# Turns of entry 1 and chunk 4 by 64-row halves, inside other small-matmul bursts

## The chip, the cores and the metric

One core of one Trainium2 chip runs the whole kernel. The metric is device time in microseconds; times shown are medians of several executions, and one execution was profiled.

Engine names in the profile: PE does matmuls (PEld its weight loads), DVE, ACT and POOL do elementwise work, SP and POOL issue DMA transfers. PE writes only to PSUM, which has eight banks here: five in the tensor `psA`, three in `psB`.

## The reference

Retention with decay per head, then a two-layer network on the tokens. Eight entries of 576 tokens, eight heads of 64; the network has 512 inputs and 2048 hidden units, on 4608 tokens.

```python
def _attn_ref(q, k, v) -> np.ndarray:
    scores = scale * np.matmul(q, k.transpose(0, 1, 3, 2))
    gamma = 1.0 - 2.0 ** (-5.0 - np.arange(H, dtype=np.float32))
    rel = pos[:, None] - pos[None, :]
    Dmat = np.where(rel >= 0, gamma[:, None, None] ** rel[None, :, :], 0.0)
    ret = scores * Dmat[None, :, :, :]
    return np.matmul(ret, v).astype(np.float32)
...
def _moe_ref(x, w_in, w_out) -> np.ndarray:
    h = x @ w_in
    g = h * (1.0 / (1.0 + np.exp(-1.702 * h)))
    return (g @ w_out).astype(np.float32)
```

## The kernel before

**Two kinds of work on PE.** The network is big matmuls: `hidden` (L765) makes one of 16 hidden tiles for a chunk of 512 tokens, 4 matmuls of 128x512; `hidden_half` (L780) does two tiles for half a chunk, 8 matmuls of 128x256; `project` (L801) adds 4 hidden tiles to 128 output rows, 4 matmuls of 128x512. Retention is small matmuls on 64-wide heads, and it runs in bursts between the big ones. Its result, scaled, goes to `xT`, which `hidden` reads.

**Retention by pieces.** Entry 0 is done in five chunks of its own (128 rows four times, then 64): chunk 4 is the short one. For a chunk n, `scores` (L463) and `mask_s` (L475) give masked scores in `sm`; `values` (L483) gives the values times scores, adds to the running state (`add_state`) and adds the part that comes from the state of earlier chunks (`add_inter`); `evac_z` (L542) copies the state out of PSUM, `evac_o` (L553) writes `xT`. The other entries are done in 21 wide steps m of 192 tokens each, in `burst(m_out, m_in)` (L626): it brings in scores and state of step m_in and takes out the values of step m_out, the values in two phases of which the second waits for the first. After it on DVE: `evac_wide` (L721) writes `xT`, `mask_wide` (L731) writes `sm`, `state_wide` (L740) adds the state to `zacc`, three operations, and a cast (ACT or DVE) makes `zw`, which the next burst's output side reads. `step(m)` is `burst(m, m+1)` and what goes with it.

**Turns.** Scores need q and k with the head dimension across partitions. From entry 2 on, a DMA transposes them (`turn_dma`, L567). For chunk 4 and the five chunks of entry 1 (n = 5 to 9), PE does it: `turn` (L562) is `transposes` (L409), 8 matmuls of 128x128 against the identity, and `evac_t` (L420), one ACT copy of 128x1024 to `qk`.

**Order.** All is written out by hand. A call records an operation on its engine's queue; each engine runs its queue in that order. The recorder (class `Rec`, L44) makes an operation wait for the last writer and the readers of what it touches, named by keys. PSUM is named by bank: "S" is `psA` banks 0 and 1, "O" bank 2, "Z" bank 3, "W" bank 4, and `psB` has ("H", 0), ("H", 1) and "U". An operation that names a bank waits for the last operation of every other engine that named the same bank, whichever columns each of them uses:

```python
        for key in ps:
            for e, o in self.ps.get(key, {}).items():
                if e != eng:
                    deps.append(o)
```

`state_wide` names "S", "W", "Z" and "O" in each of its three DVE operations (L751, L755).

`run(units, between)` (L1005) records units (one `project`, `hidden` or `hidden_half` each) and, after unit i, what `between[i]` lists; a unit with a step behind it also waits for what the step reads. The first such call (L1040) has the 16 project units of chunk 0, unit 4g + r for group g and rows r; r = 0 adds up in bank "O" over units 0, 4, 8 and 12. The next (L1047) has eight `hidden_half` units of chunk 1's first half, whose tokens come from entry 0's chunk 4 and from step 0. Loads are issued by POOL (`load`, L213) in order; from a point on each waits until the sixth load before it has landed.

## Time and profile before

| what | us |
|---|---|
| median of 3 runs (lowest, highest) | 297.17 (296.97, 298.06) |
| the profiled execution | 296.6 |
| its span | 294.8 |
| PE busy | 289.6 |
| POOL, ACT, DVE busy | 150.1, 126.6, 124.0 |
| first project unit of chunk 0 begins | 29.93 |
| first hidden unit of chunk 1 begins | 48.38 |
| first project unit of chunk 1 begins | 57.50 |

The span runs from the first instruction to the last. Lines in the timeline give start, length, engine, line, operation and tiles, array shape (rows*columns of PE in use), the moving operand's shape and a count; consecutive equal instructions are merged. Matmuls overlap: a group's length includes the tail of its last one, so the time that a group takes is read from one start to the next.

### The profile page before, as it was taken

The page shows a single profiled execution, that of the slowest core. Times are in us where ns is not written, and L with a number is a line of the kernel's source. Part 1 is how long each engine was busy: PE and PEld are TensorE (multiplying, and loading weights), DVE is VectorE, ACT ScalarE, POOL GpSimd, SP SyncE. Part 2 cuts the span into 40 slices and gives each one's busy share as a digit, 9 for nine tenths or more (in the row PEclk, how much of TensorE's full clock was granted, in tenths as well). Part 3 has the DMA queues.
Part 4 walks back from the last instruction along what each step waited for, and adds up shares of the span by engine and source line. Part 5 has one row for each costly group of instructions (what it writes and reads, how often), then busy time and mean ns, then how long its engine had stood idle before and what let it go on. Part 6 is the DMA issues. An engine that isn't in the chain of part 4 may idle for free.

```text
span 294.8 us, 7772 instructions
## 1 busy us (share of the span) xinstructions
PE 289.6 (98%) x3434; PEld 148.9 (51%) x3434; DVE 124.0 (42%) x221; ACT 126.6 (43%) x212; POOL 150.1 (51%) x202
## 2 busy tenths in 40 slices
PE   7999999999999999999999999999999999999996
PEld 3664556758544544554454544544444544444444
DVE  6899284644545443642424415235325504100012
ACT  7767338517175224531454045403650366036600
POOL 8958879999869879769968960000000000000000
PEclk9999999999999999999999999999999999999999
DMA  9999999999999999999999996008610200020012
GB/s 188 166 201 185 172 172 197 160 142 146 185 156 204 141 143 192 189 141 119 141 220 147 134 222 102 4 0 111 180 29 0 109 36 2 2 107 36 0 58 87
DMA packets 151746, 36.31 MB, mean 123 GB/s; under 512 B 141344, under 2 KB 147232, under 8 KB 151712
## 3 DMA queue, kind: packets, MB, share of 16 engines
q0 software_dynamic: 114224, 17.84, 90.9%
q1 hardware_dynamic: 37488, 17.97, 30.9%
q8 instruction: 27, 0.44, 0.6%
q14 instruction: 7, 0.06, 0.1%
HBM read 36.70 MB, written 9.44 MB: 157 GB/s over the span
## 4 chain that ended last, share of the span: by engine, by line
PE 93%; POOL 2%; DMA 2%; DVE 1%; issue 1%; POOLq 0%
PE psB L804 40%; PE psB L771 36%; PE psB L788 5%; PE psA L666 2%; PE psA L638 2%; DMA st_k<-in_k_dram 2%; PE psA L680 2%; PE psA L654 1%; PE psA L804 1%; PE psA L830 1%; POOL st_v L223 1%; POOL st_k L223 1%; PE psA L415 1%; DVE xT L557 0%; DVE sm L480 0%
## 5 line engine op out<-in xcount | busy, mean ns | idle before, releaser
L804 PE MATMUL psB<-w_out_sb,gT 128*128 128x512 bf16 x544 | 122.1, 379 | 0.0
L771 PE MATMUL psB<-xT,w_in_sb 128*128 128x512 bf16 x492 | 108.9, 379 | 0.0
L776 ACT ACTIVATE gT<-psB 128x512 bf16<-128x512 f32 x123 | 73.5, 597 | 38.7 <-PE psB L771 38.6
L804 PEld LDWEIGHTS psB<-w_out_sb,gT 128*128 128x128 bf16 x544 | 51.8, 98 | 60.3 <-DVE sm L735 0.4
L771 PEld LDWEIGHTS psB<-xT,w_in_sb 128*128 128x128 bf16 x492 | 47.4, 98 | 56.5
L724 DVE TENSOR_TENSOR xT<-psA,gq 128x768 bf16<-128x768 f32 x21 | 20.1, 957 | 113.9 <-PE psA L654 113.9
L236 POOL DMA_DIRECT2D st_k<-in_k_dram x70 | 52.9, 786 | 8.6 <-DMA st_k<-in_k_dram 3.0
L236 POOL DMA_DIRECT2D st_v<-in_v_dram x70 | 52.5, 779 | 4.5 <-DMA st_v<-in_v_dram 3.7
L813 ACT ACTIVATE osb<-psB 128x512 f32<-128x512 f32 x23 | 13.7, 597 | 71.9 <-PE psB L804 71.9
L223 POOL DMA_DIRECT2D st_q<-in_q_dram x36 | 32.3, 898 | 9.9 <-DMA st_q<-in_q_dram 6.0
L394 DVE TENSOR_TENSOR st_v<-st_v,vfac 128x512 bf16<-128x512 bf16 x38 | 24.8, 682 | 1.9 <-DMA st_v<-in_v_dram 1.9
L753 DVE TENSOR_TENSOR zacc<-zacc,psA 128x256 f32<-128x256 f32 x49 | 20.5, 418 | 7.5 <-PE psA L666 6.3
L735 DVE TENSOR_TENSOR sm<-psA,maskw 128x768 bf16<-128x768 f32 x21 | 19.9, 947 | 0.0
L788 PE MATMUL psB<-xT,w_in_sb 128*128 128x256 bf16 x128 | 15.0, 273 | 0.0
L816 DVE COPY osb<-psB 128x512 f32<-128x512 f32 x3 | 2.1, 691 | 29.7 <-PE psB L804 29.7
L788 PEld LDWEIGHTS psB<-xT,w_in_sb 128*128 128x128 bf16 x128 | 12.2, 98 | 1.7
L813 ACT ACTIVATE posi<-psB 128x512 f32<-128x512 f32 x8 | 4.8, 597 | 17.7 <-PE psB L804 17.7
L638 PE MATMUL psA<-sm,st_v 64*64 64x64 bf16 x504 | 11.7, 195 | 0.3
L666 PE MATMUL psA<-st_v,st_k 64*64 64x64 bf16 x448 | 11.8, 199 | 0.0
L666 PEld LDWEIGHTS psA<-st_v,st_k 64*64 64x64 bf16 x448 | 7.6, 105 | 8.3 <-issue 7.8
L794 ACT ACTIVATE gT<-psB 128x512 bf16<-128x512 f32 x16 | 9.4, 599 | 5.0 <-PE psB L788 5.0
L654 PE MATMUL psA<-qk,zw 64*64 64x64 bf16 x448 | 11.0, 194 | 0.0
(114 smaller groups left out, 172.2 us busy)
## 6 DMA issues: line engine op xcount, KB each, us to landing
out_dram<-osb SPq DMA_DIRECT2D x27, 256.0 KB, 4.2
st_k<-in_k_dram POOLq DMA_DIRECT2D x57, 64.0 KB, 6.7
st_v<-in_v_dram POOLq DMA_DIRECT2D x57, 64.0 KB, 6.5
st_q<-in_q_dram POOLq DMA_DIRECT2D x28, 128.0 KB, 7.9
w_out_sb<-in_moe_w_out_dram POOLq DMA_DIRECT2D x4, 512.0 KB, 11.3
out_dram<-posi SPq DMA_DIRECT2D x8, 256.0 KB
w_in_sb<-in_moe_w_in_dram POOLq DMA_DIRECT2D x3, 512.0 KB, 8.2
gT<-in_q_dram SPq DMA_DIRECT2D x2, 512.0 KB, 4.3
```

The source lines that it names most:

```text
L223: paced(R.op("POOL", lambda e, d=d, s=s: e.dma_start(d, s), w=[(nm, sl, c)], dma=(nm, sl, c), own=pace()))
L236: paced(R.op("POOL", lambda e: [e.dma_start(d, s) for d, s in parts], w=[(nm, sl, c)], dma=(nm, sl, c), parts=2, own=pace()))
L394: R.op(eng, lambda e: e.tensor_tensor(t, t, f, ALU.mult), r=[("vfac", min(b, 1))], w=[("v", sl, c)])
L666: i = e.matmul(psA[half(j), bank, off + 64 * t : off + 64 * t + 64], rows_of(st_k, m_in, g, u, h), rows_of(st_v, m_in, g, u, h), start=(t ...
L724: R.op("DVE", lambda e: e.tensor_tensor(xT[:, :, t0 : t0 + 192].rearrange("p (u j) n -> p u j n", u=2), psA[:, 2:4, 0:384].rearrange("p u ...
L735: R.op("DVE", lambda e: e.tensor_tensor(o, i, k, ALU.mult), r=["maskw"], w=[("sm", si(m))], ps=["S"])
L753: R.op("DVE", lambda e, to=to, src=src, was=was: e.tensor_tensor(to, was, src, ALU.add), r=[("zacc", (blk - 1) % 3)], w=[("zacc", blk)], p ...
L771: i = e.matmul(bank, w_in_sb[:, a, 128 * f : 128 * f + 128], xT[:, a, 512 * c : 512 * c + 512], start=(a == 0), stop=(a == 3))
L776: R.op("ACT", lambda e: e.activation(gT[c % 2][:, f, :], bank, AF.Gelu_apprx_sigmoid), w=[("gT", c % 2, f)], ps=[key])
L788: m = e.matmul(bank[:, 256 * i : 256 * i + 256], w_in_sb[:, a, 128 * (f + i) : 128 * (f + i) + 128], xT[:, a, a0 : a0 + 256], start=(a == ...
L804: i = e.matmul(bank, gT[c % 2][:, f, 128 * r : 128 * r + 128], w_out_sb[:, f, :], start=(f == 0), stop=(f == NF - 1))
L813: R.op("ACT", lambda e: e.activation(osb[m], bank, AF.Copy), w=osb_keys[m], ps=[key])
```

## The change

- `transposes`, `evac_t`, `scores`, `mask_s` and `values` use only the rows that a chunk of entry 0 has: for chunk 4, 64 rather than 128.
- A new `turn_halves` does a turn as 16 transposes, each of 64 rows by 128 columns, the two halves into two banks, with one ACT copy. A new `turn_tail` does chunk 9: the low half of q and of k into bank "O", the high half of k into bank "W", with two ACT copies.
- Turn 4 now runs with the state of chunk 3, which moves from the hidden units of chunk 0 to behind project unit 1. Scores 4 run with turn 5 behind unit 5 (before: units 3 and 5). Turn 6 runs with the values of chunk 4 behind unit 8 (before: units 7 and 5). Burst 0 moves from unit 9 to 10, step 0 from 13 to 15, with turns 7 and 8 between its two phases (before: units 12 and 15). Burst 1 moves from hidden unit 1 to 3 and has turn 9 behind it (before: unit 0); step 1 moves from 6 to 7.
- The regroupings of `w_in` columns 2 and 3 on DVE stand behind units 1 and 11 (before: 5 and 11); the memsets of chunk 4's unused rows move behind `evac_o` of chunk 3.

```diff
+        def turn_halves(n, at, x0=0):
+            bank, keys = at
+            to = bank.bitcast(BF16)[:, :, x0 : x0 + 2 * HP * 64].rearrange("p r (x n) -> p r x n", n=64)
+            def fn(e):
+                for a, t, nm, sl, c in sides(n):
+                    for hp in range(HP):
+                        for r in range(2):
+                            i = e.matmul(to[:, r, HP * a + hp, :],
+                                         t[half(r), sl, c, 128 * hp : 128 * hp + 128],
+                                         ident[half(r), half(r)], is_transpose=True)
+                return i
+            R.op("PE", fn, r=["ident"] + [(nm, sl, c) for a, t, nm, sl, c in sides(n)], ps=keys)
+            o = qk[n % NQK].ap().rearrange("p a h (r n) -> p r (a h) n", r=2)
+            R.op("ACT", lambda e: e.activation(o, to, AF.Copy),
+                 w=[("qk", n % NQK, 0), ("qk", n % NQK, 1)], ps=keys)
+
+        def turn_tail(n):
+            keys = ["O", "W"]
+            (_, tq, nmq, sl, c), (_, tk, nmk, _, _) = sides(n)
+            low = psA[:, 2, 0:256].bitcast(BF16).rearrange("p (a h n) -> p a h n", a=2, n=64)
+            high = psA[:, 4, 384:512].bitcast(BF16).rearrange("p (h n) -> p h n", n=64)
...
+            R.op("PE", fn, r=["ident", (nmq, sl, c), (nmk, sl, c)], ps=keys)
+            R.op("ACT", lambda e: e.activation(qk[n % NQK][:, :, :, 0:64], low, AF.Copy),
+                 w=[("qk", n % NQK, 0), ("qk", n % NQK, 1)], ps=["O"])
+            R.op("ACT", lambda e: e.activation(qk[n % NQK][:, 1, :, 64:128], high, AF.Copy),
+                 w=[("qk", n % NQK, 1)], ps=["W"])
+
+        halves_s = (psA[:, 0:2, :], ["S"])
+        halves_z = (psA[:, 3:5, :], ["Z", "W"])
...
-        def burst(m_out, m_in, cast="DVE"):
+        def burst(m_out, m_in, cast="DVE", middle=()):
...
+            for i, n in enumerate(middle):
+                turn_halves(n, halves_s, 2 * HP * 64 * i)
             if m_out is not None:
                 def phase_y(e):
...
-        constants_third(0, 1)
         hidden_part(2, 0, 256)
         hidden_part(3, 0, 256)
         hidden_part(0, 256, 384)
         values(3, third[0], "values")
         evac_o(3, third[0])
+        constants_third(0, 1)
...
-            if f == 7:
-                values(3, third[0], "state")
-                evac_z(3)
...
         def tail_turn():
             turn(4)
+            values(3, third[0], "state")
+            evac_z(3)
             scale_v(4)
...
-            {1: [(tail_turn,)], 3: [(intra, 4)], 5: [(turn, 5), (tail_out,), (regroup, 2)],
-             7: [(scale_v, 5), (turn, 6)], 8: [(scale_v, 6)], 9: [(burst, None, 0, "ACT")],
-             11: [(regroup, 3)], 12: [(turn, 7)], 13: [(step, 0, False)], 14: [(scale_v, 7)], 15: [(turn, 8)]})
+            {1: [(tail_turn,), (regroup, 2)], 5: [(intra, 4), (turn_halves, 5, halves_z), (scale_v, 5)],
+             8: [(turn_halves, 6, halves_s), (tail_out,), (scale_v, 6)],
+             10: [(burst, None, 0, "ACT")], 11: [(regroup, 3)],
+             14: [(scale_v, 7)], 15: [(step, 0, False, "DVE", (7, 8)), (scale_v, 8)]})
         turn_step(3)
         turn_step(4)
         run(units_half(1, 0),
-            {0: [(turn, 9, True), (scale_v, 8)], 1: [(burst, None, 1, "ACT")],
-             2: [(scale_v, 9)], 6: [(step, 1)]})
+            {3: [(burst, None, 1, "ACT"), (turn_tail, 9), (scale_v, 9)], 7: [(step, 1)]})
```

More of the change, by code (lines that the diff above doesn't have):

```diff
@@ L410, in transposes @@
             to, key = turned(at)
+            N = ROWS[n] if n < NC else P
             def fn(e):
@@ L414, in fn @@
                     for hp in range(HP):
-                        i = e.matmul(to[:, a, hp, :], t[:, sl, c, 128 * hp : 128 * hp + 128],
-                                     ident.ap(), is_transpose=True)
+                        i = e.matmul(to[:, a, hp, 0:N], t[0:N, sl, c, 128 * hp : 128 * hp + 128],
+                                     ident[0:N, 0:N], is_transpose=True)
                 return i
@@ L421, in evac_t @@
             to, key = turned(at)
-            R.op("ACT", lambda e: e.activation(qk[n % NQK].ap(), to, AF.Copy),
+            N = ROWS[n] if n < NC else P
+            R.op("ACT", lambda e: e.activation(qk[n % NQK][:, :, :, 0:N], to[:, :, :, 0:N], AF.Copy),
                  w=[("qk", n % NQK, 0), ("qk", n % NQK, 1)], ps=[key])
@@ new lines, in turn_tail, with fn @@
+        def turn_tail(n):
[3 more added lines that the diff above has]
+            high = psA[:, 4, 384:512].bitcast(BF16).rearrange("p (h n) -> p h n", n=64)
+            def fn(e):
+                for hp in range(HP):
+                    cols = slice(128 * hp, 128 * hp + 128)
+                    i = e.matmul(low[:, 0, hp, :], tq[half(0), sl, c, cols],
+                                 ident[half(0), half(0)], is_transpose=True)
+                for hp in range(HP):
+                    cols = slice(128 * hp, 128 * hp + 128)
+                    for r, to in ((0, low[:, 1, hp, :]), (1, high[:, hp, :])):
+                        i = e.matmul(to, tk[half(r), sl, c, cols],
+                                     ident[half(r), half(r)], is_transpose=True)
+                return i
+            R.op("PE", fn, r=["ident", (nmq, sl, c), (nmk, sl, c)], ps=keys)
[3 more added lines that the diff above has]
+                 w=[("qk", n % NQK, 1)], ps=["W"])
@@ L469, in fn @@
                     for j in range(2):
-                        i = e.matmul(at[:, j, 2 * (hp % 2) + hp // 2, 0:N],
-                                     now[half(j), 1, hp, :], now[half(j), 0, hp, 0:N])
+                        i = e.matmul(at[0:N, j, 2 * (hp % 2) + hp // 2, 0:N],
+                                     now[half(j), 1, hp, 0:N], now[half(j), 0, hp, 0:N])
                 return i
@@ L476, in mask_s @@
             N = ROWS[n]
-            m = mask[:, 0:N].unsqueeze(1).to_broadcast([P, 2 * HP, N]) if n != 3 else mask3
-            o = sm[n % 3].rearrange("p a h c -> p (a h) c")[:, :, 0:N]
-            i = at.rearrange("p a h c -> p (a h) c")[:, :, 0:N]
+            m = mask[0:N, 0:N].unsqueeze(1).to_broadcast([N, 2 * HP, N]) if n != 3 else mask3
+            o = sm[n % 3].rearrange("p a h c -> p (a h) c")[0:N, :, 0:N]
+            i = at.rearrange("p a h c -> p (a h) c")[0:N, :, 0:N]
             R.op("DVE", lambda e: e.tensor_tensor(o, i, m, ALU.mult),
@@ L492, in av @@
                         u, t, j = h // 4, h // 2 % 2, h % 2
-                        i = e.matmul(po[half(s2), a, 0:N], st_v[:, sl, c, 64 * h : 64 * h + 64],
-                                     sm[n % 3][:, j, 2 * t + u, 0:N],
+                        i = e.matmul(po[half(s2), a, 0:N], st_v[0:N, sl, c, 64 * h : 64 * h + 64],
+                                     sm[n % 3][0:N, j, 2 * t + u, 0:N],
                                      start=(a == 0), stop=(c == 0), skip_group_check=True)
@@ L979, in tail_out, with step @@
             load_entry(NST)
-        def step(m, into=True, cast="DVE"):
+        def step(m, into=True, cast="DVE", middle=()):
             b, i = 1 + m // 3, m % 3
-            burst(m, m + 1 if into and m + 1 < NWIDE else None, cast)
+            burst(m, m + 1 if into and m + 1 < NWIDE else None, cast, middle)
             if m > 1:
```

## The prediction

> **What bounds the kernel now.** I read the page's busy shares and chain of waits first, then the waits of TensorE (PE), then the timeline stretch by stretch.

> ```profile
> PE 289.6 (98%) x3434; PEld 148.9 (51%) x3434; DVE 124.0 (42%) x221; ACT 126.6 (43%) x212; POOL 150.1 (51%) x202
> ...
> PEclk9999999999999999999999999999999999999999
> ...
> PE 93%; POOL 2%; DMA 2%; DVE 1%; issue 1%; POOLq 0%
> ```

> PE is busy 98% of the span at full clock, and the chain that sets the end is PE for 93%. Busy alone can hide stalls, so the waits of PE over the whole span are the second view (microseconds in all, times, longest), with the row of the long rest after 57.5 us (length, then busy PE, PEld, DVE, ACT, POOL):

> ```profile
> PE psB L870 <- DVE lnh L281: 1.2, 1, 1.2
> ...
> PE psA L434 <- DMA st_k<-in_k_dram: 0.3, 1, 0.3
> ...
> 57.50:294.80 237.30, 234.66 (x2722) 116.00 (x2719) 83.92 (x140) 90.76 (x152) 100.64 (x135) 1.00 1.11 109
> ```

> The view lists only waits of the first microseconds; in 237.30 us after 57.5 PE is idle 2.64, at changes of matmul shape. So PE waits for nobody later on: each microsecond taken from its stream moves the end forward, and each microsecond in which it waits moves the end back. Nothing later can absorb a delay. Everything that changes lies before 57.5 us, so I price each PE group as the time it inserts between the big matmuls.

> **What a turn and a small burst cost.** Columns: start, length, engine, line, what.

> ```profile
> 31.66 0.39 PE L415 MATMUL psA<-ident,st_q 128*128 128x128 bf16 x4
> 31.89 0.39 PE L415 MATMUL psA<-ident,st_k 128*128 128x128 bf16 x4
> 32.11 1.89 PE L804 MATMUL psB<-w_out_sb,gT 128*128 128x512 bf16 x8
> 32.31 1.02 ACT L422 ACTIVATE qk<-psA 128x1024 bf16<-128x1024 bf16 x1 [1.58 <-PE psA L415]
> 33.93 0.29 PE L470 MATMUL psA<-qk 64*128 64x64 bf16 x8
> 34.15 1.04 PE L804 MATMUL psA<-w_out_sb,gT 128*128 128x512 bf16 x4
> ```

> A full turn inserts 32.11 - 31.66 = 0.45 (0.056 a transpose) and no gap, because its shape 128*128 is that of its neighbours. Six of them are 2.69. A big matmul takes 0.216, so the eight at 32.11 end at 33.84; the scores start at 33.93 and big work resumes at 34.15: 0.32 inserted, of which 0.09 is entering the small shape and about 0.10 leaving it. The eight 64*128 matmuls between them start within 0.10, two at a time: about 0.03 a pair. A half-row turn of 16 transposes has exactly this shape, so 8 pairs, 0.25, against 0.45. Turn 4 (8 transposes of one half) and turn 9 (4, then 4 pairs) have no row; their bounds are 0.03 and 0.056 per step, and I take 0.03, the row of the same shape: 0.25 each.

> The chunk-4 state and the tail:

> ```profile
> 22.77 0.32 PE L506 MATMUL psA<-gT,st_k 128*64 128x64 bf16 x8
> 23.02 7.08 PE L771 MATMUL psB<-xT,w_in_sb 128*128 128x512 bf16 x32
> ...
> 36.12 0.39 PE L415 MATMUL psA<-ident,st_k 128*128 128x128 bf16 x4
> 36.43 0.32 PE L493 MATMUL psA<-sm,st_v 128*64 128x64 bf16 x8
> 36.58 0.29 PE L529 MATMUL psA<-qk,zs 128*64 128x64 bf16 x8
> 36.80 1.90 PE L804 MATMUL psB<-w_out_sb,gT 128*128 128x512 bf16 x8
> ```

> State inserts 0.25 (0.15 of work, 0.10 leaving) plus 0.09 entry = 0.34. Values and inter insert 36.80 - (36.12 + 0.22) = 0.46, of which 0.27 is their work. So turn 4, state, scores, turn 5, turn 6 and tail are 0.45 + 0.34 + 0.32 + 0.45 + 0.45 + 0.46 = 2.47 before.

> After, they are three bursts. Turn 4 + state: 0.09 + 0.25 + change of shape 0.10 + 0.15 + 0.11 = 0.70. Scores + turn 5: 0.09 + 0.14 + 0.10 + 0.25 + 0.11 = 0.69. Turn 6 + tail: 0.09 + 0.25 + 0.10 + 0.14 + 0.10 + 0.15 + 0.11 = 0.94 (the values now use 64 rows, a shape other than inter's, so one more change). Together 2.33: gain 0.14. The change between 64*64 and 64*128 inside a burst has no row; its bounds are 0 (as between equal shapes) and the 0.10 of a change to 128*128. I take 0.10. [...]

> **Burst 0 and the wait of unit 12.** Project units are 4 big matmuls, 0.87 each.

> ```profile
> 39.85 1.03 PE L804 MATMUL psB<-w_out_sb,gT 128*128 128x512 bf16 x4
> 40.90 0.26 PE L666 MATMUL psA<-st_v,st_k 64*64 64x64 bf16 x8
> 41.48 1.90 PE L804 MATMUL psB<-w_out_sb,gT 128*128 128x512 bf16 x8
> 41.60 0.42 DVE L750 COPY zacc<-psA 128x256 f32<-128x256 f32 x1 [0.76 <-PE psA L666]
> 42.06 0.88 DVE L753 TENSOR_TENSOR zacc<-zacc,psA 128x256 f32<-128x256 f32 x2
> 43.21 1.03 PE L804 MATMUL psA<-w_out_sb,gT 128*128 128x512 bf16 x4
> ```

> The burst was due at 40.71 + 0.09 and started at 40.90, held by scale_v(6); after, that scale is long done: gain 0.10. But unit 12 (43.21) writes bank "O", and state_wide names "O" in its three DVE operations, so unit 12 waits for the third. That ends at 42.94, 1.46 after PE resumed. Before, two units stood between (1.73): hidden, 0.27 to spare. Now burst 0 comes after unit 10 and one unit (0.87) stands between: 1.46 + 0.06 - 0.88 = **0.64 stall**.

> **Step 0 with turns 7 and 8 inside.**

> ```profile
> 44.52 1.03 PE L804 MATMUL psB<-w_out_sb,gT 128*128 128x512 bf16 x4
> 45.48 0.32 PE L638 MATMUL psA<-sm,st_v 64*64 64x64 bf16 x16
> 45.63 0.23 PE L654 MATMUL psA<-qk,zw 64*64 64x64 bf16 x8
> 45.94 0.26 PE L638 MATMUL psA<-sm,st_v 64*64 64x64 bf16 x8
> 46.03 0.23 PE L654 MATMUL psA<-qk,zw 64*64 64x64 bf16 x8
> 46.20 1.90 PE L804 MATMUL psB<-w_out_sb,gT 128*128 128x512 bf16 x8
> 46.32 0.96 DVE L724 TENSOR_TENSOR xT<-psA,gq 128x768 bf16<-128x768 f32 x1 [0.88 <-PE psA L654]
> ```

> Before, step 0 inserts 46.20 - 45.39 = 0.81, a quarter of it PE waiting for itself between its two phases, and the two turns 0.90: 1.71. After: entry 0.09, first phase 0.22, change 0.10, turns 0.25 and 0.23, change 0.10, second phase 0.16 (45.94 to 46.20 less the leaving), leaving 0.11: 1.26, the turns filling that self-wait. Gain 0.45. Two waits come with it.

> First, both turns name the one key "S", though they write different columns. Turn 8 must therefore wait until ACT has copied turn 7. The copy takes 1.02 and starts right after the turn's last transpose ends (32.28 to 32.31 above; a small one lasts 0.19): 0.19 + 0.04 + 1.02 + 0.06 - 0.03 = **1.28 stall**. Behind turn 8 the second phase queues, and behind it every big matmul. The copy has a strided output now; bounds 1.1 to 1.5.

> Second, step 0 moves from unit 13 to unit 15, directly ahead of chunk 1's first hidden unit, which reads the xT that evac_wide(0) writes. That evacuation runs from 46.32 to 47.28 when PE would resume at 46.20. Two units and turn 8 covered it; now PE resumes at 47.28 + 0.06: **1.14 stall**. scale_v(7), now ahead of it on DVE, is done by then.

> **Burst 1 with turn 9.**

> ```profile
> 51.24 4.54 PE L788 MATMUL psB<-xT,w_in_sb 128*128 128x256 bf16 x40
> 51.37 1.33 DVE L753 TENSOR_TENSOR zacc<-zacc,psA 128x256 f32<-128x256 f32 x3 [2.89 <-PE psA L666]
> ```

> The turn leaves its own place (0.45) and costs 0.35 in the burst: gain 0.10. But turn_tail names "O" and "W", recorded after state_wide(1), which names them in all three DVE operations. It could start where PE resumed, 51.24, and waits until 52.70 + 0.06: **1.52 stall**. Queued behind it: the rest of chunk 1. Later steps keep their distance: step 2 now has six project units (5.2) behind step 1, where it had a hidden unit more; the DVE work between them, an evacuation (0.96), a mask, two state adds (0.44 each) and a cast, is well under that.

> **The memsets.**

> ```profile
> 17.01 0.41 PE L521 MATMUL psA<-qk,zq 64*64 64x128 bf16 x8
> 17.27 0.27 DVE L340 MEMSET st_v<- 64x256 uint32 x1
> 17.57 0.69 DVE L557 TENSOR_TENSOR xT<-psA,gq 128x512 bf16<-128x512 f32 x1
> 17.81 0.39 PE L882 MATMUL psA<-xT,w_in_sb 128*128 128x128 bf16 x4
> 18.32 0.40 PE L882 MATMUL psB<-xT,w_in_sb 128*128 128x128 bf16 x4
> ...
> 18.65 0.71 POOL L223 DMA_DIRECT2D st_v<-in_v_dram  x1
> ...
> 31.08 0.69 DVE L394 TENSOR_TENSOR st_v<-st_v,vfac 128x512 bf16<-128x512 bf16 x1 [1.31 <-DMA st_v<-in_v_dram]
> ```

> evac_o(3) could start at 17.47 and starts at 17.57 behind the memset; PE, idle from 18.03, takes up its result at 18.32. Gain 0.10. The price is that POOL issues chunk 4's loads 1.2 later and, with the DVE constants 0.8 later, entry 1's too. The transfer that POOL issued at 18.65 landed at 31.08, so 12 us of queued transfers cover it; with that cover gone, turn 4, now at about 31.2, would wait up to 1.2. q and k precede that v in the queue, so they are in by then.

> **The sum.** Gains 0.14 + 0.10 + 0.45 + 0.10 + 0.10 = 0.89. Stalls 0.64 + 1.28 + 1.14 + 1.52 = 4.58. Net 3.7 slower. The profiled execution took 296.6 itself (span 294.8 and 1.8 around it), which gives 300.3; its median of three runs is 297.17, 0.6 above, which gives 300.9. I say 300.8. Bounds: gains 0.5 (single-half turns at 0.056) to 1.3 (no drain inside bursts), stalls 4.0 to 5.2: 2.7 to 4.7 slower, 299.3 from the lower base to 301.9 from the upper.

> **Rivals.**
> 1. Not slower: the waits are real but a later stretch paced by loads absorbs them, PE arriving late at data that was late too. For it: POOL, which issues the loads, is still busy 100.64 of the 237.30 us after 57.5. It decides from 4.6 us of later PE waits for loads. Against: the waits view names none after the start. It would leave the gains alone: 297.2 - 0.9 = 296.3. Chance 0.05.
> 2. The change doesn't do what it says: the half transposes don't run in pairs, each taking 0.03 for itself. Then four turns cost 0.25 more each: 301.8. Against: the score row of the same shape pairs. Chance 0.06.
> 3. The clock drops. Stalls of 1.28 and 1.14 follow each other within 2 us. Against: waits of 1.2 and 0.3 stand in the first microseconds and the clock reads 9 in every slice. A drop to half for as long as the three late stalls together (3.9 us) costs another 2.0: 302.8. Chance 0.04. [...]

> **How the numbers follow.** The forecast has 0.83, the rivals 0.15, and 0.02 is left for what I have not seen. I take 299.3 to 302.0, which is the bounds and the second rival, and leaves out rivals 1 and 3. About 0.5% (1.5 us) is what a measurement can tell from no change. Slower by more: the forecast less its thin lower tail, rivals 2 and 3, 0.90. Within: 0.07, most of it rival 1. Faster by more: 0.03, for even free turns gain only 2.69 + 0.66 for two bursts saved, less than the stalls.

> **What would show it.** In the changed profile, PE's waits should name four new rows between 40 and 55 us: DVE zacc before unit 12 (0.6), ACT qk in the middle of step 0 (1.3), DVE xT before the first hidden unit (1.1), DVE zacc before turn 9 (1.5). The 16 half transposes should last 0.4 from first start to last end. Units after 61 us should run 3.7 later with gaps unchanged. The forecast is wrong if any of the four is missing, or if PE after 61 us has caught up.

## The result, and the profile after

| | before | after |
|---|---|---|
| median, us | 297.17 (296.87 to 298.06, 6 executions) | 301.96 (300.24 to 304.35, 6 executions) |
| profiled execution: time, span, us | 296.6, 294.8 | 300.24, 298.5 |
| ratio after to before, 95% interval | | 1.0163 [1.0135, 1.0192] |

The changed kernel is slower by 1.6%. Its six executions are not alike. Two took 300.24 and 300.29 us, both with a span of 298.5 and a mean granted clock of 1.0. The other four took 301.63, 302.29, 303.15 and 304.35, all with a mean clock of 0.994. The profiled execution is the first of the two. Its trace holds no record of the clock, so its page has no row for it; but in the timeline below 32 hidden matmuls take 3.67, some 0.11 each, as 40 take 4.54 in before, so this trace shows what the change does while the clock holds. The page of after, busy shares and chain of waits:

```profile
PE 284.9 (95%) x3435; PEld 148.2 (50%) x3470; DVE 124.0 (42%) x221; ACT 126.8 (42%) x213; POOL 150.2 (50%) x202
...
PE 92%; issue 2%; DVE 2%; DMA 2%; ACT 1%; POOLq 0%
```

PE still sets the end. The fall from 98% to 95% is only partly idle time: 3470 weight loads stand beside 3435 matmuls, so the records of 35 matmuls are missing, and a missing one can read as a gap. The waits of PE over the whole span of after (us in all, times, longest):

```profile
PE psB L854 <- issue: 2.5, 16, 0.2
PE psA L459 <- DVE zacc L803: 1.4, 1, 1.4
PE psB L920 <- DVE lnh L281: 1.2, 1, 1.2
PE psA L440 <- ACT qk L446: 1.1, 1, 1.1
PE psB L838 <- DVE xT L774: 1.1, 1, 1.1
...
PE psA L854 <- DVE zacc L803: 0.5, 1, 0.5
```

The first row is the missing records: 16 gaps of 0.16, released by nothing. Rows 2, 4, 5 and 6 are new and are the four waits that the prediction named. Row 3 stood in before too. The timeline of PE in after shows where they lie (start, length, engine, line, what, idle time before):

```profile
43.37 1.04 PE L854 MATMUL psA<-w_out_sb,gT 128*128 128x512 bf16 x4 [0.48 <-DVE zacc L803]
...
46.93 0.32 PE L686 MATMUL psA<-sm,st_v 64*64 64x64 bf16 x16
...
47.24 0.29 PE L440 MATMUL psA<-ident,st_q 64*128 64x64 bf16 x8
47.37 0.28 PE L440 MATMUL psA<-ident,st_k 64*128 64x64 bf16 x8
48.77 0.29 PE L440 MATMUL psA<-ident,st_q 64*128 64x64 bf16 x8 [1.12 <-ACT qk L446]
...
50.50 3.67 PE L838 MATMUL psB<-xT,w_in_sb 128*128 128x256 bf16 x32 [1.07 <-DVE xT L774]
...
56.19 0.23 PE L459 MATMUL psA<-ident,st_q 64*128 64x64 bf16 x2 [1.45 <-DVE zacc L803]
...
61.24 2.97 PE L854 MATMUL psB<-w_out_sb,gT 128*128 128x512 bf16 x13 [0.16 <-issue]
```

An idle time in brackets is short of what a wait costs the stream, since the last matmuls before it are drawn with a modelled end. Measured from start to start, less what the matmuls between insert, the four waits are 0.64 (unit 12), 1.28 (turn 8), 1.14 (the first hidden unit) and 1.5 (turn 9): 4.56 together. The row at 61.24 starts the long rest; its first matmul is one of the missing records, so that rest starts at 61.24 - 0.22 = 61.02, where before had 57.50. One window over it (length, busy PE, PEld, DVE, ACT, POOL, granted clock, DMA share, GB/s):

```profile
61.02:298.50 237.48, 231.04 (x2699) 116.25 (x2720) 84.77 (x140) 90.17 (x151) 96.90 (x130) 1.00 1.04 107
```

It takes 237.48, against 237.30 before, with 2720 weight loads against 2719. Nothing after 61 us takes any of the delay back.

### The profile page after: what moved, and what is told of

It is laid out like the page before. It is cut to its first block, busy times and chain, and to the rows that moved or that the text cites. A ratio compares the mean times of both kernels' runs of the same rounds, so it can differ in the third digit from the quotient of the medians.

```text
span 298.5 us, 7808 instructions
## 1 busy us (share of the span) xinstructions
PE 284.9 (95%) x3435; PEld 148.2 (50%) x3470; DVE 124.0 (42%) x221; ACT 126.8 (42%) x213; POOL 150.2 (50%) x202
## 4 chain that ended last, share of the span: by engine, by line
PE 92%; issue 2%; DVE 2%; DMA 2%; ACT 1%; POOLq 0%
PE psB L854 39%; PE psB L821 35%; PE psB L838 5%; PE psA L714 2%; PE psA L686 2%; DMA st_k<-in_k_dram 2%; PE psA L728 1%; PE psA L702 1%; PE psA L854 1%; PE psA L880 1%; PE psB L932 1%; DVE zacc L803 1%; PE psA L440 0%; PE psA L541 0%; ACT qk L446 0%
## 5 line engine op out<-in xcount | busy, mean ns | idle before, releaser
L854 PE MATMUL psB<-w_out_sb,gT 128*128 128x512 bf16 x523 | 117.6, 379 | 2.8 <-issue 2.5
L821 PE MATMUL psB<-xT,w_in_sb 128*128 128x512 bf16 x481 | 106.9, 379 | 1.3 <-issue 1.0
L223 POOL DMA_DIRECT2D st_q<-in_q_dram x36 | 32.3, 896 | 6.0 <-DMA st_q<-in_q_dram 3.1
L394 DVE TENSOR_TENSOR st_v<-st_v,vfac 128x512 bf16<-128x512 bf16 x38 | 24.9, 682 | 0.9 <-DMA st_v<-in_v_dram 0.9
```

Of the source, the lines that this page charges most:

```text
L223: paced(R.op("POOL", lambda e, d=d, s=s: e.dma_start(d, s), w=[(nm, sl, c)], dma=(nm, sl, c), own=pace()))
L394: R.op(eng, lambda e: e.tensor_tensor(t, t, f, ALU.mult), r=[("vfac", min(b, 1))], w=[("v", sl, c)])
L821: i = e.matmul(bank, w_in_sb[:, a, 128 * f : 128 * f + 128], xT[:, a, 512 * c : 512 * c + 512], start=(a == 0), stop=(a == 3))
L854: i = e.matmul(bank, gT[c % 2][:, f, 128 * r : 128 * r + 128], w_out_sb[:, f, :], start=(f == 0), stop=(f == NF - 1))
```

## The experiments

Nine runs were made, in three groups, each beside the kernel before on the same chip. Two questions were put. Do the four waits add up to the loss, each by its own size? And why did four of six executions take 1.3 to 4.1 more than the other two?

**The changed kernel again, unchanged (again).** The trace of after had missed the slower kind of execution.

> The changed kernel once more, on one chip with its variants. Theory 1 (four waits add 4.6 us, the gains give 0.9 back, and the further time of some executions is a lowered clock): undisturbed executions have a span of 298.5 us at clock 1.0, the others 1 to 4 us more at 0.994. Theory 2 (the waits themselves vary from run to run): long executions show clock 1.0.

Measured: 302.54 (300.32 to 302.96, 6 executions), ratio 1.0175 [1.0148, 1.0201]. Five of the six have a clock of 0.994 and spans of 300.1 to 301.2; the sixth has 1.0 and 298.5 again. The profiled one is of the five. Its clock by slices, then its PE timeline:

```profile
PEclk9999998899999999999999999999999999999999
```

```profile
49.74 0.29 PE L440 MATMUL psA<-ident,st_q 64*128 64x64 bf16 x8 [1.12 <-ACT qk L446]
...
51.47 5.08 PE L838 MATMUL psB<-xT,w_in_sb 128*128 128x256 bf16 x32 [1.07 <-DVE xT L774]
```

The waits are those of after, within a hundredth. But the 32 matmuls of the first hidden units take 5.08 instead of 3.67: **1.4 more for the same work**. This trace keeps each change of the granted clock; windows cut at those times (columns as above, the clock third from the end) show one stretch at half speed, and what PE did in the stretch of equal length ahead of it:

```profile
47.57:50.99 3.42, 1.71 (x74) 1.06 (x72) 0.95 (x2) 2.59 (x4) 3.42 (x6) 1.00 1.37 174
50.99:54.40 3.41, 2.93 (x14) 2.09 (x15) 1.02 (x2) 0.82 (x2) 3.41 (x5) 0.50 1.72 263
54.40:57.81 3.41, 2.73 (x68) 2.20 (x65) 0.59 (x2) 1.79 (x3) 3.41 (x6) 1.00 2.24 139
```

The clock is at half for 3.41 us and then whole again; 3.41 / 2 / 301 is the 0.006 that the mean lacks. The rest of the 2.7 by which this span exceeds after's is mostly the start: here PE waits 1.0 for the first rows of w_in, which after's trace does not have.

```profile
PE psA L821 <- DMA w_in_sb<-in_moe_w_in_dram: 1.0, 1, 1.0
```

**Without the wait for ACT's copy (no_copy_wait).** Both half turns run on PE first and their copies follow, so that turn 8 waits for no copy of turn 7.

```diff
             for i, n in enumerate(middle):
-                turn_halves(n, halves_s, 2 * HP * 64 * i)
+                turn_halves(n, halves_s, 2 * HP * 64 * i, copies)
+            for copy in copies:
+                copy()
```

> Both turns of step 0 stand on TensorE before either copy, so turn 8 no longer waits for the copy of turn 7. Theory 1: span 298.5 - 1.28 = 297.2 us at clock 1.0. If the two idle stretches in step 0 (1.1 and 1.1 us, 0.5 us of small matmuls between) lower the clock together, every execution is at 1.0 and the median falls to about 299.0. Rival (any idle stretch of about 1.4 us lowers it, the one before turn 9 too): clock 0.994 still turns up in about as many executions, median about 300.5.

Measured: 299.19 (298.94 to 299.83), ratio 1.0074 [1.0058, 1.009]. The clock is 1.0 in all six executions, the spans 297.2 to 298.0. The lowest span is 1.3 under after's 298.5, the size of the wait (1.28); the profiled one, of 298.0, waits 0.7 for w_in at its start, as again did. Counted from the first project unit, which leaves the start out, its burst 1 comes after 53.65 - 30.23 = 23.42, where after has 54.09 - 29.38 = 24.71: 1.29 less. In its list of PE's waits the copy is gone and the other three are as they were:

```profile
PE psA L465 <- DVE zacc L812: 1.4, 1, 1.4
...
PE psB L847 <- DVE xT L783: 1.1, 1, 1.1
...
PE psA L830 <- DMA w_in_sb<-in_moe_w_in_dram: 0.7, 1, 0.7
PE psA L863 <- DVE zacc L812: 0.5, 1, 0.5
```

Two findings in one run: the wait costs its own size, and with it the drop of the clock is gone as well.

**Without the wait of turn 9 (no_tail_wait).** turn_tail is recorded inside burst 1, between PE's matmuls and state_wide, so it no longer waits for the three DVE operations.

```diff
+            if tail is not None:
+                turn_tail(tail)
...
-            {3: [(burst, None, 1, "ACT"), (turn_tail, 9), (scale_v, 9)], 7: [(step, 1)]})
+            {3: [(burst, None, 1, "ACT", (), 9), (scale_v, 9)], 7: [(step, 1)]})
```

> Turn 9 stands ahead of the DVE state adds in the record, so TensorE does not wait for them. Theory 1: span 298.5 - 1.5 = 297.0 us at clock 1.0. If step 0's two stretches lower the clock, 0.994 still turns up here, median 299 to 300.5. Rival (the stretch before turn 9 lowers it): always 1.0, median 298.8.

Measured: 302.11 (300.38 to 302.78, 5 executions), ratio 1.0165 [1.0141, 1.019]; the clock is 0.994 in four. The expectation of the span was missed: the one execution at full clock has 298.6, not 297.0. The timeline of this kernel, its PE, its DVE and its ACT:

```profile
61.11 1.05 PE L840 MATMUL psB<-xT,w_in_sb 128*128 128x256 bf16 x8 [1.29 <-DVE st_v L394]
```

```profile
58.26 1.33 DVE L805 TENSOR_TENSOR zacc<-zacc,psA 128x256 f32<-128x256 f32 x3 [6.87 <-ACT qk L470]
59.51 0.95 DVE L787 TENSOR_TENSOR sm<-psA,maskw 128x768 bf16<-128x768 f32 x1
60.38 0.68 DVE L394 TENSOR_TENSOR st_v<-st_v,vfac 128x512 bf16<-128x512 bf16 x1
```

```profile
57.15 0.60 ACT L468 ACTIVATE qk<-psA 128x512 bf16<-128x512 bf16 x1 [0.33 <-PE psA L464]
57.77 0.39 ACT L470 ACTIVATE qk<-psA 128x256 bf16<-128x256 bf16 x1
```

The order is merely turned round. Now state_wide, which names the same banks, waits for ACT's two copies (they end at 58.16), and behind its operations and the mask DVE has scale_v(9), whose result the unit at 61.11 needs. The wait is 1.29 there, in place of 1.45 at turn 9. Giving the turn keys of its own was not tried: DVE and ACT would then use one bank with no order between them, and no run here shows what comes of that.

**Without any of the four (all_four).** The two edits above together, burst 0 back at its old place behind unit 9 with scale_v(6) ahead of it, and step 0 behind unit 14 in place of 15.

```diff
-             8: [(turn_halves, 6, halves_s), (tail_out,), (scale_v, 6)],
-             10: [(burst, None, 0, "ACT")], 11: [(regroup, 3)],
-             14: [(scale_v, 7)], 15: [(step, 0, False, "DVE", (7, 8)), (scale_v, 8)]})
+             8: [(turn_halves, 6, halves_s), (scale_v, 6), (tail_out,)],
+             9: [(burst, None, 0, "ACT")], 11: [(regroup, 3)],
+             14: [(step, 0, False, "DVE", (7, 8)), (scale_v, 7), (scale_v, 8)]})
```

> All four waits removed: both turns before both copies, turn 9 ahead of the state adds, burst 0 behind unit 9, step 0 behind unit 14. What is left of the waits is about 0.3 us before the unit of the next chunk that reads xT. Theory 1: the gains alone remain, span 298.5 - 1.28 - 1.5 - 0.64 - 0.87 = 294.2 us at clock 1.0 in every execution, 0.6 us under the kernel before. Rival (the bursts themselves cost more than priced): not under 294.8.

Measured: 297.79 (297.32 to 298.96, 12 executions), ratio 1.0035 [1.0023, 1.0048]; the clock is 1.0 (twice 0.999) in all twelve, the spans are 295.5 to 297.2. Three waits are gone and the fourth is the moved one of the run before, which this run was expected not to have: PE's waits hold

```profile
PE psB L849 <- DVE st_v L394: 1.3, 1, 1.3
```

That row is the size of the difference between the expected 294.2 and the lowest span, 295.5.

**Turn 9 back in its own place (turn9_back).** As all_four, but turn 9 is again a full turn after the first hidden unit, as before.

```diff
-            {3: [(burst, None, 1, "ACT"), (turn_tail, 9), (scale_v, 9)], 7: [(step, 1)]})
+            {0: [(turn, 9, True)], 1: [(burst, None, 1, "ACT")], 2: [(scale_v, 9)], 6: [(step, 1)]})
```

> Turn 9 back in its own place as 8 full transposes behind hidden unit 0, burst 1 and step 1 where they were before; the other three waits removed as in all_four. Neither TensorE nor DVE now waits around turn 9. Theory 1: bursts 6.7 us and 0.3 us of wait for xT against 7.1 us before, 0.1 us from the memsets: span 0.5 us under that of the kernel before, clock always 1.0. Rival (something else in the shared bursts costs what all_four lost): 0.5 to 1 us over it.

Measured: 296.93 (296.13 to 298.38, 12 executions) against 297.17, ratio 1.0000 [0.9985, 1.0014]. The loss is gone, but the 0.5 expected in its place is not there. One new small wait, at turn 9, is on its timeline:

```profile
49.18 0.38 PE L417 MATMUL psB<-ident,st_q 128*128 128x128 bf16 x4 [0.29 <-ACT posi L872]
```

ACT clears turn 9's bank late, since the two copies of the half turns, 1.02 each, now stand ahead of that on ACT. From start to start this wait is 0.45, and the one for xT ahead of it 0.27: 0.72 lost, about what the bursts gain: from the first hidden unit of chunk 0 (19.17) to the long rest (57.52) this kernel takes 38.35, and before 57.50 - 19.23 = 38.27.

**The same with turn 9, burst 1 and step 1 later (turn9_late).** The last run, to remove that 0.45.

```diff
-            {0: [(turn, 9, True)], 1: [(burst, None, 1, "ACT")], 2: [(scale_v, 9)], 6: [(step, 1)]})
+            {2: [(turn, 9, True)], 3: [(burst, None, 1, "ACT")], 4: [(scale_v, 9)], 7: [(step, 1)]})
```

> As the run before with turn 9 back in its own place, but turn 9, burst 1, the scale of chunk 9 and step 1 stand two, two, two and one units later in chunk 1, so that turn 9's bank has been evacuated when PE comes to it. Own theory (gaps are set by who evacuates what last, and each removed gap moves the end by its own size): the gap of 0.45 before turn 9 is gone from PE's list; one of about 0.27 before the first hidden unit stays. The stretch from the first project unit to chunk 1's first project unit gets about 0.45 shorter than with turn 9 ahead of hidden unit 1, so the span lies about 0.45 under that of the run before it, some 0.4 under the kernel before, the median near 296.7, ratio 0.9985 (0.997 to 1.0), clock 1.0 in every execution. Rival (the delay is only passed on to step 1, which now stands nearer to burst 1): a new row of 0.3 to 0.5 at step 1's state or xT, span as in the run before, ratio 1.000.

Measured: 297.10 (296.27 to 297.86, 12 executions) against 297.17, ratio 0.9996 [0.998, 1.0012]. Neither theory alone held. The wait at turn 9 is gone, but PE's waits have another, smaller one, at the unit ahead of step 1:

```profile
PE psB L847 <- DVE st_v L394: 0.2, 1, 0.2
```

It is again scale_v(9), behind the state adds and the mask on DVE. No version that ran beats the kernel before by a measurable amount.

**Only step 0 moved (no_xt_wait), only burst 0 moved (no_unit_wait).** Each is a part of all_four's diff, on the changed kernel.

```diff
-             14: [(scale_v, 7)], 15: [(step, 0, False, "DVE", (7, 8)), (scale_v, 8)]})
+             14: [(step, 0, False, "DVE", (7, 8)), (scale_v, 7), (scale_v, 8)]})
```

> Only step 0 moves, to behind unit 14, so that one unit covers its xT; the copy wait (1.28) and the wait before turn 9 (1.5) stay. Theory 1: span 297.6 us at clock 1.0. If the lowered clock needs both stretches of step 0, it never shows: median 299.4. Rival (the copy wait alone does it): 0.994 in most executions, median over 300.5.

Measured: 299.78 (299.73 to 300.4, 4 executions), ratio 1.0094 [1.0076, 1.0113], spans 297.9 to 298.6 where 297.6 was expected, and a clock of 1.0 in all four. The wait for the copy is still there, the wait for xT is not, and the drop is gone. Counted from the first project unit, burst 1 comes after 53.57 - 29.71 = 23.86, 0.85 less than the 24.71 of after, so the stretch is as short as expected and the profiled span's missing 0.3 is a later start (29.71 against 29.38).

```diff
-             8: [(turn_halves, 6, halves_s), (tail_out,), (scale_v, 6)],
-             10: [(burst, None, 0, "ACT")], 11: [(regroup, 3)],
+             8: [(turn_halves, 6, halves_s), (scale_v, 6), (tail_out,)],
+             9: [(burst, None, 0, "ACT")], 11: [(regroup, 3)],
```

> Only burst 0 moves back to behind unit 9, with scale_v(6) ahead of the tail's evacuation. Theory 1: the 0.64 us before unit 12 are gone, span 297.9 us at clock 1.0; both stretches of step 0 stay, so 0.994 stays in most executions and the median is 301 to 302. Rival (that wait is hidden anyway): the fastest executions stay at 298.5.

Measured: 300.9 (300.53 to 301.41, 4 executions), ratio 1.0126 [1.0103, 1.0149]. Two executions have a clock of 1.0 (spans 298.7 and 298.8) and two 0.994 (299.4 and 299.6). The 0.5 row before unit 12 is gone from the list, yet the spans at full clock are not 0.6 below 298.5. The start hides it, and the timeline shows it: the first project unit and the first phase of step 0 stand at

```profile
29.34 1.03 PE L854 MATMUL psA<-w_out_sb,gT 128*128 128x512 bf16 x4
...
46.24 0.32 PE L686 MATMUL psA<-sm,st_v 64*64 64x64 bf16 x16
```

That is 16.90, where after has 46.93 - 29.38 = 17.55: the wait's removal gives its own size, 0.65. And the drop does not hang on it.

**One long wait in place of two (copy_twice).** Step 0 moved as in no_xt_wait, and ACT copies turn 7 twice over.

```diff
-            R.op("ACT", lambda e: e.activation(o, to, AF.Copy),
+            for _ in range(2 if n == 7 else 1):
+                R.op("ACT", lambda e: e.activation(o, to, AF.Copy),
```

> As no_xt_wait, but ACT copies turn 7 twice, so that TensorE has one idle stretch of about 2.3 us instead of 1.3. Theory 1, if what counts is idle time in all within some 3.4 us: 0.994 shows in some executions, span 298.6 at clock 1.0 and 300 to 301 at 0.994. Rival (two stretches are needed, or one of 3.4 us): always 1.0, median 300.4.

Measured: 301.62 (300.73 to 302.43, 4 executions), ratio 1.0151 [1.0125, 1.0177]; spans of 299.3 and 298.9 at a clock of 1.0, and 300.6 and 300.4 at 0.994. One idle stretch of 2.2 brings the drop back, in two of four:

```profile
PE psA L440 <- ACT qk L447: 2.2, 1, 2.2
```

**What stood ahead of the drop.** The kernels that have the copy wait and the xT wait within 3 us (after, again, no_tail_wait, no_unit_wait) dropped in 15 of 21 executions; those with only one wait of up to 1.5 at a time, or none (no_copy_wait, no_xt_wait, all_four, turn9_back, turn9_late), in 0 of 46. What PE did ahead of half clock can be read where a trace has a record of the clock, in windows of the 3.41 that half clock lasted in again. The window ahead of half clock and the one behind it, beside again's above: first no_tail_wait, then no_unit_wait, then the end of before, where the record has full clock from 4.42 to 294.55 (a window that holds PE's last matmuls, and the idle tail):

```profile
48.17:51.59 3.42, 1.39 (x39) 1.17 (x40) 1.55 (x2) 1.92 (x2) 3.42 (x5) 1.00 1.49 241
51.59:55.00 3.41, 3.41 (x18) 2.45 (x17) 0.00 (x0) 1.20 (x2) 3.41 (x6) 0.50 2.15 178
```

```profile
45.88:49.30 3.42, 1.74 (x74) 1.06 (x72) 0.51 (x1) 2.59 (x4) 3.42 (x6) 1.00 1.26 213
49.30:52.71 3.41, 2.90 (x14) 2.09 (x15) 1.05 (x2) 0.85 (x2) 3.41 (x5) 0.50 1.85 227
```

```profile
291.13:294.55 3.42, 1.27 (x19) 0.98 (x16) 0.85 (x2) 0.00 (x0) 0.00 (x0) 1.00 0.24 80
294.55:296.00 1.45, 0.00 (x0) 0.00 (x0) 0.00 (x0) 0.00 (x0) 0.00 (x0) 0.50 0.00 0
```

And windows of two executions that did not drop, copy_twice and no_xt_wait:

```profile
47.98:51.39 3.41, 1.90 (x39) 1.06 (x40) 1.29 (x2) 2.69 (x4) 3.41 (x6) 1.00 1.73 226
51.39:54.81 3.42, 3.42 (x44) 2.89 (x45) 0.87 (x2) 2.05 (x4) 3.42 (x5) 1.00 1.71 169
54.81:58.22 3.41, 1.88 (x70) 1.62 (x70) 2.65 (x5) 1.45 (x3) 3.41 (x6) 1.00 2.10 140
58.22:61.63 3.41, 3.41 (x113) 2.96 (x110) 0.08 (x1) 3.03 (x6) 3.41 (x6) 1.00 2.29 126
```

```profile
53.22:56.63 3.41, 1.96 (x70) 1.52 (x69) 2.29 (x5) 1.30 (x3) 3.41 (x6) 1.00 2.11 175
56.63:60.04 3.41, 3.41 (x80) 2.92 (x80) 0.44 (x1) 3.10 (x7) 3.41 (x6) 1.00 3.35 96
```

Windows in which PE was busy 1.27, 1.39, 1.71 and 1.74 are followed by half clock; these of 1.88, 1.90 and 1.96 are not. But little work in 3.41 us does not bring the drop by itself, as after's profiled execution shows. Its trace has no clock record (the view writes 1.00 for that), but the 32 matmuls that fill the second of these stretches run at full speed, 3.67 for the 32 as above:

```profile
47.08:50.49 3.41, 1.22 (x72) 0.90 (x64) 1.01 (x2) 2.60 (x3) 3.41 (x6) 1.00 1.64 240
50.49:53.90 3.41, 3.40 (x32) 3.05 (x32) 0.55 (x1) 1.77 (x3) 3.41 (x6) 1.00 2.08 196
```

The first stretch, with 1.22 busy, was emptier than each of the four windows that were followed by half clock. So the two waits together, or one idle stretch of 2.2 as in copy_twice, came with the drop in some executions and not in others; what decides between two executions of one kernel was not shown. The window need not be empty: one with PE busy 1.74 of 3.41 was followed by half clock.

## Why the prediction was right and where it was wrong

**The four waits: right, each in place and size.** Foreseen were 0.64, 1.28, 1.14 and 1.52; the trace has 0.64, 1.28, 1.14 and 1.5. Removal shows the first (0.65, no_unit_wait), the second (1.29, no_copy_wait) and the third (0.85 with some 0.3 left over, no_xt_wait). The fourth was not shown by removal, since it moved; that it is a wait on shared banks is shown by where it went.

**The gains: about right.** The stream up to the long rest came 61.02 - 57.50 = 3.52 later, with 4.56 of waits in it, so the gains are 1.04 where 0.89 was said. 0.10 of this is luck: the first transposes stand at 5.28 in after and at 5.38 in before, ahead of anything that changed. The memsets' 0.10 is in the rest: PE takes up the result of evac_o(3) at 18.11 in place of 18.32, which is 0.11 beyond that earlier start. The 16 half transposes from 47.24 end near 47.65, 0.4 as foreseen, so they do run in pairs and the second rival fell. Step 0's first phase and the change to the turn's shape take 47.24 - 46.93 = 0.31; less the phase's own 0.22 this is 0.09, where the prediction took 0.10 between bounds of 0 and 0.10. So the change of shape inside this burst was not free. The upper bound of the gains, 1.3, calls such a change a drain and leaves out four of them; no run shows a drain, and what the trace shows in its place is this 0.09. But none of this shows as a shorter time. In turn9_back, which keeps nearly all the gains and drops the four waits, two leftovers of 0.72 eat what the bursts gain; the two half-turn copies, one right behind the other on ACT, are behind the larger. The prediction priced those copies for turn 8 alone, not for what ACT does next.

**Nothing absorbed later: right.** The long rest takes 237.48 against 237.30; the first rival fell.

**The sum: right for an execution at full clock.** 296.6 + 3.7 is 300.3; the three such executions of the changed kernel, of after and of again, took 300.24, 300.29 and 300.32.

**The clock: wrong, and with it the time.** The step that failed is the third rival, "The clock drops", which got a chance of 0.04. It happened in 9 of 12 executions, so the median, 301.96, is one with the drop in it: 300.3, 1.4 for the hidden units at half clock, and 0.3 that may come from a start like that of again, of which no trace was taken. That it comes out at the upper end of the stated range, 302.0, is luck: that end stood there for longer waits, smaller gains or the second rival, and none of these happened. What was held against it, that waits of 1.2 and 0.3 stand in the first microseconds and the clock reads 9 in every slice, misreads what it rests on. The timeline of before shows what stands there:

```profile
1.19 3.69 PE L870 MATMUL psB<-idle 128*128 128x512 bf16 x9 [1.19 <-DVE lnh L281]
```

Nine filler matmuls take 3.69, some 0.41 each, where the same shape takes 0.216 later, so PE ran at about half speed there. The trace's first record of full clock is at 4.42; ahead of that record the page draws full speed. So the matmuls right behind the 1.2 ran at half speed, and that wait can say nothing against a drop; the 0.3 is short. In the three traced drops PE was busy 1.39 to 1.74 in the 3.41 ahead of half clock: that is what 1.28 and 1.14, with only some 0.5 of small matmuls between them, left of it. The prediction had these waits; it noted that the two "follow each other within 2 us" and did not add them. The price was not far off: 2.0 for a drop to half as long as the stalls, against 1.4 measured in again, as the drop there lasted 3.41 at 0.50 and a part of it was a wait anyway.

**Left open.** Of the executions of the kernel before that ran beside the experiments, 3 of 51 also had a mean clock of 0.989 or 0.994 and took about 304; no trace of one was taken, so where their clock fell is not known. Nor is it settled what of PE's work decides: the small matmuls use a part of the array (64*64 and 64*128 in the timeline, against 128*128), and PE's ends are modelled, so the 1.39 to 1.74 are busy time as the profile draws it.

## What to carry to other kernels

Add up the waits that an edit puts on PE close together, not only each by itself: here two waits of 1.1 and 1.3 within 3 us came with a drop of the clock in 15 of 21 executions, which cost 1.4 more than their sum in again, and putting one unit of four big matmuls between them, which also covered one of the two, ended it (0 of 4 in no_xt_wait). One key for two banks, or one key for two users of one bank, turns work that shares nothing into a queue; recording the users in another order only moves the wait to whoever comes second. Where PE never waits, moving small work into bursts saves only what it inserts (some 0.9 of 297 here), so check first who evacuates what, and what else stands in that engine's queue.

## What of the hardware was not expected

```profile
5.28 1.06 PE L497 MATMUL psA<-ident,st_q 128*64 128x128 bf16 x16
```

```profile
5.28 0.64 PE L497 MATMUL psA<-ident,st_q 128*64 128x128 bf16 x16 [0.48 <-DVE st_q L275]
```

The next sixteen, at 7.18 in again and at 7.05 in after, take 0.64 in both. The page's row of the clock reads full speed there in again, and after's page has no such row, so the spacing of the matmuls has to be read instead.
